# A phase's maxima turned by four VectorE transpositions instead of one TensorE transposition, with 24 tiles of exponentials and a new issue table

## The chip, the cores and the metric

The kernel runs on one core of one Trainium2 chip. The metric is device time in microseconds (us); lower is better. Before the change the median of three runs is 1726.11 us (1723.06 to 1726.36).

## What is computed

A layer normalisation of x (2048 tokens by 512) feeds two branches: softmax attention with 32 heads of 16 channels, and a gated feed-forward network of inner width 1792 (SwiGLU). The output is x plus the attention's result times a SiLU of the feed-forward's result. All is float32.

```python
xn = _layernorm(x)                                   # 2048 x 512
q, k, v = split(xn @ wqkv)                           # 32 heads, 16 channels
p = softmax(q @ k.T * 16 ** -0.5)                    # 2048 x 2048 for each head
s = (p @ v) @ wo
h = silu(xn @ w1) * (xn @ w3)                        # 2048 x 1792
g = silu(h @ w2)
out = x + s * g
```

## The kernel before

**Phases.** Two heads are a pair (`p`, 16 pairs) and 1024 query columns are a `half` (2 of them), so there are 32 phases. In each phase the kernel goes over all 2048 keys. Before a phase's exponentials can be taken, the row maximum of every query has to be known: `max_unit` (L380 on) multiplies 128 queries by 512 keys on one half of the array (L388) and VectorE reduces the 512 scores in PSUM to one maximum for each query (L390, tile `mp`). A phase has 64 of these products, 32 on each half of the array.

**Bringing the maxima to the exponentials.** `max_rows` (L393 on) is a generator with four steps, run once for each phase. Step 1: VectorE reduces the four part maxima of each query to one (`mx`, 128 queries by 16). Step 2: ScalarE writes them negated to `nm`. Step 3: TensorE transposes `nm` into a PSUM bank (L403, 16 rows by 128), ScalarE copies the rounded part to `mh` (L406) and VectorE writes the rest to `ml` (L407). Step 4: four transfers on SyncE's queue (SP, L414) write `mh` and `ml` of the two heads into rows 62 and 63 of each 64-row half of `qs`, the tile of queries. With these two rows the product of keys and queries already has the maximum subtracted.

**Exponentials and values.** `scores` multiplies keys by queries on one half of the array (L626), and ScalarE takes the exponential into a tile `pt` (L629), of which there are `PTS` = 23. `values` (L639) multiplies four such tiles with the values into the bank `pv`, 16 matmuls of 128 columns by 512 in the trace for two chunks of keys and 8 for one. The feed-forward network's products (L857, 4032 half-array products) run between them. All products but the values' go to seven PSUM banks in turn; `take` hands out the bank that the planner expects to be free first. GpSimd (POOL) splits and multiplies in SBUF for the feed-forward network (L320, L321, L727, L742, L744).

**The order of work.** The program is written out ahead of time: the string `ORDER_OF_ISSUE` has a letter for each piece of TensorE work, and the loop at the end of the kernel issues the pieces in that order. `f`, `m` and `s` are half-array products of the feed-forward network, the maxima and the scores (a capital is the upper half of the array), `v` is one chunk of values, `o` a tile of the final projection. In the table before, `r` is a `v` ahead of which `second` issues step 3 and step 4 of a phase's maxima, and `R` is that alone. A model in the kernel (`mod`) keeps an expected time for every engine; `small` uses it to choose where in the program the steps of `max_rows` are put. After the program is built the order on each engine is fixed, and a late engine is waited for.

Of the kernel before, what the change touches and what calls it, by code (L numbers as in the profile page):

```python
# [9 lines left out]
F32 = mybir.dt.float32  # L10
# [7 lines left out]
P = 128  # L18
# [17 lines left out]
PTS = 23  # L36
# [14 lines left out]
    "MfSfMffSMffSSffMfSffMfSfFFMMfffMMfsFfsFfFSffmFsFFfMsFfMFfmmFFmMFvvSmmFsFfSffMsFfmFFsFfMsfFSfMfFfMsFS"  # L51
    "ffMFfFffMFSfFfMfSfSfmsfFmFFsFmFsFfFmSfmFfFmMfFMmvvFsMMsFsfFfFmFsfFMsfFFmsFmFFfSffMfFfMMfFMfMfMsvvSmf"
    "MsfFfSFfmSFffSFmFmfFmSFffSFmFfFfMmfFMFmvvSmFmSffSfFmFmfFSfFsmFfFFsfFmFFfMfMfMfMFfFMmvvvsMsMfffFmFfSM"
    "fsFsFFffMsFFfmSFfFfFfmMFMfsMvrFSmmsFsFsFmFffFMfsFfMsfFfSMfSffMFfFfSffMfFMfSFFffMfSfsMfSFfmFsfFFmSFfm"
    "FsFfmFmFsFMsvvMsMmSsvFmsFMmmSvvmSSfMfFfSffMSffFmFFsSfmFFmFfsFfFSffMFmMmvvMsSffFfMfSfMfSFfmFFsmFfSfFF"
    "msFFsfFFsFmsMvvsMSmMsvMmfMSfmMFvvMFssfMffSfMfSFfmSFffSmfFsFFmSfFFmsFfFFffMfSfMffSMfFFsmFfFmfSfFSfFmF"
    "sfFFmFsfSFsFmvrvvMsSffMFfSffMSffFmSSFffFmsFffMFSffMsFfsFMfFmFFfsmFmMvFvsMsMMsvMmsMfFSSfvSmMsMsvSmffS"
    "MffSFfMfSfMffSmsfFmSFfSfmsFfFSmFfFFmFsFmfSsFFfmFfSFfmFsFmSfFMfFffFmMMmvvMsfMfSMsvMssMMsvmSFfMsFsfFFm"
    "fFSmFsFfmFFsFfMsfFsFmFSfFfMfFsfSmFsFfFMfSffFMsFfMfFffMfMMffMMmvvvSmmMSmvvSmmSFfSffFFmsFFmFsFfFmSfSfF"
    "mfFfMSsfFFmfSfFmFsFFmFsfFFmSffFsFMffMMmvrfMFMsMmMfvvvfMSfMfSffSfMffSfMFsfmFFsFmSfsFfFFmfFmSfFFsFmFsF"  # L60
    "fmFsFFmsFFFmFssFSsvvSmsSsSvvSmSmmSvmSFmsFFfFsFmfSFfMsfFfSFmfSfFMfSfSfFmfMFfFFmMvvsMsMsfFfFmFfMsfFsFM"
    "ffSfFMfSfFmSfFsFfFfmMMsvrsMMssMvMsSfMffSFffMFfmSfSFfmFFsFfmFsFfMsFfFfFmSFmmMvvmSsMMmvvsMsFFmFmFsFfFs"
    "fFSmfFSfMfFfSfMffSfFSmfFFffFFMSffMfFSffSmfsMfsFFmFsFmFsFmFfFMfmFMmvvMsMmfSfSvmSsMSmvMsfMfSfFSffMFfmS"
    "fSFfFmFfsFmsFfFSFmfSfFmfFfFMSFfffFSFmsFfmFFmsFfsFSffMFFffmFFfMmMmvvvvmMSsMsvSmsFmFmFFsFsFfFfSmFfSfMf"
    "FffMSffFsMfFfFMffSFfFMfSfSfFMfsmsFfFmsFfFMsFmFfSfmFfFFmfMMmvvvmSMssSvrvSmmFsFsFmFFsfFFfMsfFfMfSfFfMS"
    "mfFfSfFfMFsfMFMsvvvmFsFmsFFmsFFffSfMfSFfmSfFmFsFMffFSfSfMmvmSMffMsSvsMSfSffMFfFfSmfFsFMfsFfFsMFfFmsF"
    "sFfMFfffFMfSffSFMffMsfSFfFmFsfFMsfFmFsFFfFmFmFmSmvvvSmsSsSvvSsMmMsvfSfMSfMfSffMfSfFfSfMFfsFFsmFfsFMf"
    "sFfFMsFfmFSFfffMFMfssMvsFSFMmMsvrvMsfSMfffSfMSffMFffSmssfFMFfsFmfFsFFmfSFmfFSffSFmSFfFmsFFfmFsFfMsFM"
    "fFffSmFSmvvSmMsMmvvmMSfmSSfvSmmSMsvSmsFFmsFFfFmSffFSmfFSfMfSffFMsfFMfsFFfMfsFfFsMFffSMfSffFsMFfmFFsm"
    "FfFFfFFMmMmvvvMssmFsFsFmFffFFsMfFsMfFfSffMSffMFffSmFfSfFfMSfFmSfFfFmSfFmfFFfMmmMvvrMsmFFfSsvvvSmsFFm"  # L70
    "FsfFFfFmSfmFfSfFFsmFmFfSFfFsmFFsFfmSfFmFsFFsfFfSSfMsvvSssSmMvvvFmsFmFsFmFsFfFsFFmSffFMsfFfMSfMffFMff"
    "MSsvMfmSMfSsvmSsMSmvmSfSMfSfFffMmFfSfsFmFfFSFfFsmFfSmFffSFffmFFMFfSfmFsfFFsMFfFsmFsfFMsfFmFSfFfMfFmS"
    "fMmvvmMsSMsvsMFmFsFsmFFfFsfFMsfFfMSfFfMfSffMFsfFfMmFfMMmvvvMmmSsMvrMsSffMFfSffMSfFfmSffFSmFsFfMsfFFF"
    "msFmmFfFFmMFmvvsMsMfFfSffMsFfMfFFsmFsFFfsFmSFffMfSfffFfMFfSMffSfMfFsFFmFsFmSffFFmFsFmFfFmmFsMvvSmSmS"
    "mvfMMsSfSmvmSmSSmvmSFmFsFfFsfMFsfMfFsFMffSFfmSFffMsFfMFfsMfFMmvvMmmMsSvrmSfSmFFfFsFmsFFsFmfFSMfSfFfm"
    "SfFMfSfFffMfMFmMsvvvsMMffSfFfSfMSffFsMFfsFmFFsfFsMFffMsFfFsFffFMfMfFSffSfMSffFmSfFfSmFsFfFmFsFmFFsFm"
    "FsmFvvvvsMSmFffFsFfFSmfFSfMfSffFmSfFmFsFFffMFFfmSSmvvvMsFsfMfsFfFMfsFfFFmsFMfsFMffFFsMfFffMfSsMvmSfS"
    "MfFffSfMSffFsMfFfSMffFSfFmsFfMFsFffMsFFfFsfFSsSmvvSmmFSSsvvvSmmSMsvSfMfSfMffSfFSfMffSfMsfFmFsfMfSFfF"
    "sFmFsfMFsfFMfsFFsfMFfFsFmsFfFMfsFfMsFMfFffFsSMmvmMsMmSvvmMsSMmvrmSfSMffSFffMSffFsMFfSfMffSFfmFsFmFfF"
    "FsFmsFfFmSfFFsFmFsFfmSFfmFsFfFfMfMSfmsMSSvmFmvmSSmmMvvmFMmFmMmvvvmFsFFmsFFsFmFffSmFSffMfSfFmFSfSffMf"  # L80
    "SFffMSffFMfFsfMSfFfFmsFMfFfsSfFmMvMssMsMvrsMsFFsFmFmFfFsFfmFFmSffFFsFmSffFSfmFSfmFSffFmFSfFmFfmFmFmS"
    "vvMmsSSmvsMmFFssFsFFmfFfFfMfSfMFsfFfMSfFmFfsFfMMmvFvMsMmSsvfMMfSsMsvMsfSffMSffMFffSFmmFSfffSMFfsfFmF"
    "fsfFmFFsFFfMFsFFfmsFFSfmfSFfMFfsFfmFSfFmFMffmFsMvvMsSsmMvSmmFMmFmvvrSmSfmFfFsFFmSffMFsFffMfSfMfSFsFf"
    "fMffFfFFMSffMfSfSfMfSfFmFsfmFSFfsmFFfsFFssFFsmFvvvvsMsMmSvMsFfsMSffFfMfSfMfFsMFfsSfFfMfFFsmFsFFfmFfF"
    "fMfFSfMfSfSfmFffSFmFFsmsFfFFmSFffFmFFmmSmvvmSmSmSvvmSMmMsvvsMsFFmFsFfFmFsFfMfFsfMSfMfFfSfMfFsfFfFMfS"
    "ffMfSfSfFMFfsmFsFfMsfFmFsFFfMfSfmFmFfFsFsMvvSfSfsMfSvvvsMMfSffFSffMsfFfMSfFsFFmsFfFmsFFFfsmFfFMfFfSm"
    "SfFFmFfSfmFfSmFSfFfFmsFFmfFSsFfsMvvvmSsSSsvvmSsMsSvrsMffSMSfFffMfSfFmSfSfFmFFsFfmfFSmFfFsFfFfmFfMSff"
    "FSmFsFfMfFsFmFsFSfmFsFfMfMfFFfFmmSmvvvMsmFfSFfsFFmfSFffMsFFsMfFffSMfSfFfMsfFMfSffMFffFMmmMvvvMsmmMff"
    "MvFvSfMfSMfSfffSMffSmSfFfMsfFFMfsFFsfMsfFFMfFsfMFsffFMsFsFfMfFsFmFsFFmsFfMfFMsfFmMvvvmSSFfmffSFfMfSf"
    "FmSffFSmfFFfSmsFFmFsfFFFmsfFSfMFsFfmfSfFMFsffMSfFfFFmsFmMsvvvrvfSMfSffMfSffSMfSFfmFSffMSfFffMsFFfsMf"  # L90
    "sFFsMFffSFmFfFsmFFsfFmSFfFmsFsfFFFsmFSsvvvSmSssSvvmSmSSmvSmFsSmFmvmSfFSmFsFfFmfFsFmFsFFmsFfFsFMffSFm"
    "SfFfmFSffMFssFFfSfsFMmvvSssMmSvvSsSsMmvvMsSmmSvMssFFmsFmFfFsFfMfSfFfMFsMffSfFfMsFfMFfmFFMfSmvvmSMssf"
    "FfFFmMfFsfFFsFmfFSmFFsfMFfMfffSMffSmSvmMmSSmvrsMmFSfFfFsFmFsfFMffSMffSMfFfSfFmsFfFFsFfSsMsvvvFFmsMfs"
    "SfFFffMSffFmfSMffFSfmFFsFsfFMfFFfMffSfMSffFFfSmfFsFmFsFmfSFfFmsFFmfFfMmFSFmvvmSsmFFsFfFfsMFfFsfMFsFf"
    "MsfFMfSfFfFmfSMfmSFvMmSsmMvvmMsMmMvvfSfMSffMfSfSfmFsFfFmFFsfMsFmFFfsFfFMmMfFfmSvvsMMsMsvmSfSMffFSffM"
    "SffFmSfsFFmFmfFSfFsFmSFfFfffmFFMSFfMfFfsFmsFfFFsmsFfFMsfFmFSfFfmFMsfSfMmvrvSmSmmsMvvMMSmvmFFsmFFssFm"
    "FFffSfMSffFmSFfMfsFfFMfsFSfMFmvMsFSmMsvMfMsMsfSFvssMSmfFfmSffFSmFFfsMSffFMfsFFmfSFffMfMFmmMvvvsMSfMf"
    "FffSfMfSFfmSfFfSFmFfFsmFfSFmfFsfFFmFfMfSfFSfmFSffFsFMfFssFmFfFmFsFMfFfFmSfsSvvvSmSmmMvrsMSfMfFfSffMf"
    "SFfmFsfFMssFfFMfSFfmFsFfMFsffMSFffMfFfsSMmvsSmMsFMvvvvMffSMfSffMfSffSfMfSfmSFfMfFsfMfFSsFfFmSfFfmFFs"
    "fMsFFffSFmSfFmsFfFFmsFsFfFmFFmMmvvMmsMMmvvFsFmsfFmFSfFFsmSffFFfMSfsFfMfFsFmFsfFFFmsfFSFmFfSfmFSffMsF"  # L100
    "ffFMMfMfffMFMfMmvvvMFsmfSffSfMfSffSMfFsFmFFsFfSmfFSfmFfFFsmFfFsMffFSFmSffFmSfFmFsFfFMfsFMfSmvMmmMSsv"
    "vmMSmMsvrSmFmFssFFsFmfFFfFsMfsFFmFffSFmFsmFfFsFFfMsfFfMSfFfFsFfSmSsFvvvvmFsFmFsFmFsfFfSFmFsFfMsfFMfS"
    "fSffFfMMfsMFvsMFMfSfsSvSmMfsfSffMmFfsFFfSFmSfFfmFsFfMfFFsFmSmvvSsFSmSmvFvmSMfSfFMmvvmSSmsffFmSfFfMsF"
    "fFsMFsFfsMfFfMfSfFFffMsMmMvvMsfMfSfFMffSfsFMfFSffMFsfmFsFfFSmfFfsFFmFfFFMSfffMsfFfFSmsFFmFsfFFsMFfFs"
# [1248 lines left out]
```

## Time and profile before

| | before |
|---|---|
| median of 3 runs | 1726.11 us (1723.06 to 1726.36) |
| the profiled execution | 1724.77 us, of which 1723.0 us are its span |
| TensorE (PE) busy | 1715.4 us, 13236 matmuls |
| VectorE (DVE) busy | 1418.7 us |
| ScalarE (ACT) busy | 1240.6 us |
| GpSimd (POOL) busy | 766.5 us |

The times of a matmul's end are modelled in the trace, so for TensorE the starts are what is read: the distance between the starts of two products is what the first one really held up. A row of the timeline that joins several instructions gives the start of the first.

### The profile page before, as it was taken

Reading aid. Unit: us, or ns where it says so; the run is one execution under the profiler, and the core shown is the slowest. Engines: PE = TensorE matmul, PEld = TensorE weight load, DVE = VectorE, ACT = ScalarE, POOL = GpSimd, SP = SyncE. Lnnn points to the kernel's source line nnn. Section 1 sums busy time; section 2 is a strip of 40 time slices with the busy share of each in tenths; the row PEclk is TensorE's granted clock in tenths of the full one; section 3 lists DMA queues with packets and bytes.
Section 4 is the critical chain, followed back from the end, with each engine's and each line's share of the span. In section 5 each row is a group of like instructions: output and inputs, shape, how many; then the busy total and the mean of one; then the engine's idle time right before and its main releaser. Section 6 shows DMA issues by size and latency. Waiting matters only on the chain.

```text
span 1723.0 us, 35685 instructions
## 1 busy us (share of the span) xinstructions
PE 1715.4 (100%) x13236; PEld 1099.0 (64%) x13236; DVE 1418.7 (82%) x2349; ACT 1240.6 (72%) x2440; POOL 766.5 (44%) x793
## 2 busy tenths in 40 slices
PE   9999999999999999999999999999999999999998
PEld 7877766666556666666666666656666666564466
DVE  7567989898889889888789897799878888888835
ACT  4223787778877787787887778777787778778952
POOL 4102744365546542654464706661666156621201
PEclk9999999999999999999999999999999999999999
DMA  8757213232332312233322303133413223130632
GB/s 282 248 204 206 65 46 66 53 70 64 73 113 59 66 53 61 55 66 95 100 64 55 80 19 91 57 75 94 94 53 67 57 66 94 30 112 20 214 121 99
DMA packets 147374, 155.37 MB, mean 90 GB/s; under 512 B 42368, under 2 KB 101760, under 8 KB 144224
## 3 DMA queue, kind: packets, MB, share of 16 engines
q1 hardware_dynamic: 146336, 152.04, 32.2%
q8 instruction: 104, 1.70, 0.4%
q10 hardware_dynamic: 864, 1.05, 0.2%
q14 instruction: 70, 0.57, 0.1%
HBM read 107.97 MB, written 44.02 MB: 88 GB/s over the span
## 4 chain that ended last, share of the span: by engine, by line
PE 98%; DVE 1%; DMA 0%; issue 0%; POOL 0%; ACT 0%; SPq 0%; DVEq 0%; ACTq 0%; POOLq 0%
PE f L857 28%; PE pv L639 28%; PE m L388 16%; PE e L626 16%; PE m L506 2%; PE e L194 2%; PE e L198 2%; PE e L196 2%; PE o L194 1%; PE o L198 1%; PE o L196 1%; PE m L479 0%; PE m L403 0%; DMA qs<-ml 0%; PE o L1088 0%; DVE wr L1035 0%
## 5 line engine op out<-in xcount | busy, mean ns | idle before, releaser
L390 DVE TENSOR_REDUCE mp<-m 128x1 f32<-128x512 f32 x2048 | 1287.1, 683 | 204.3 <-PE m L388 130.0
L629 ACT ACTIVATE pt<-e 128x512 f32<-128x512 f32 x2048 | 1072.3, 606 | 280.0 <-PE e L626 161.2
L626 PE MATMUL e<-qs,ks 64*128 64x512 f32 x2048 | 709.0, 408 | 0.6 <-DMA qs<-ml 0.5
L388 PE MATMUL m<-ks,qs 62*128 62x512 f32 x2048 | 708.2, 416 | 0.1
L639 PE MATMUL pv<-pt,vt 128*17 128x512 f32 x4096 | 497.4, 595 | 0.0
L388 PEld LDWEIGHTS m<-ks,qs 62*128 62x128 f32 x2048 | 334.4, 184 | 158.7 <-DVE mp L390 52.5
L626 PEld LDWEIGHTS e<-qs,ks 64*128 64x128 f32 x2048 | 343.1, 184 | 125.8 <-DVE mp L390 33.7
L639 PEld LDWEIGHTS pv<-pt,vt 128*17 128x17 f32 x4096 | 90.2, 96 | 220.0 <-issue 210.2
L857 PE MATMUL f<-xth,wh 64*128 64x512 f32 x488 | 175.4, 392 | 0.0
L857 PE MATMUL f<-xtl,wh 64*128 64x512 f32 x488 | 174.6, 392 | 0.0
L857 PE MATMUL f<-xth,wl 64*128 64x512 f32 x488 | 173.2, 394 | 0.0
L742 POOL TENSOR_TENSOR h<-g,h 128x512 f32<-128x512 f32 x56 | 72.2, 1289 | 187.7 <-ACT h L738 187.6
L857 PE MATMUL f<-wh,hs 64*128 64x512 f32 x496 | 153.7, 393 | 0.0
L857 PE MATMUL f<-xtl,xeh 64*128 64x512 f32 x408 | 148.9, 392 | 0.0
L857 PE MATMUL f<-xth,xel 64*128 64x512 f32 x408 | 145.8, 395 | 0.0
L857 PE MATMUL f<-xth,xeh 64*128 64x512 f32 x408 | 142.4, 391 | 0.0
L857 PE MATMUL f<-xeh,hs 64*128 64x512 f32 x400 | 127.6, 393 | 0.0
L321 POOL TENSOR_TENSOR wl<-wr,wh 128x512 fp32r<-128x512 f32 x92 | 118.6, 1290 | 7.7
L320 POOL TENSOR_SCALAR wh<-wr 128x512 fp32r<-128x512 f32 x92 | 57.3, 622 | 121.2 <-PE f L857 61.2
L321 POOL TENSOR_TENSOR xel<-wr,xeh 128x512 fp32r<-128x512 f32 x76 | 98.0, 1290 | 6.3
L857 PEld LDWEIGHTS f<-xth,wl 64*128 64x128 f32 x488 | 85.4, 185 | 7.3 <-issue 3.4
L857 PEld LDWEIGHTS f<-xth,wh 64*128 64x128 f32 x488 | 86.9, 185 | 4.9 <-issue 0.8
(184 smaller groups left out, 2007.6 us busy)
## 6 DMA issues: line engine op xcount, KB each, us to landing
wr<-in_B_w_dram SPq DMA_DIRECT2D x168, 256.0 KB
qs<-qk SPq DMA_DIRECT2D x186, 64.0 KB
ks<-qk SPq DMA_DIRECT2D x90, 128.0 KB
qk<-sh SPq DMA_DIRECT2D x32, 256.0 KB
qk<-sl SPq DMA_DIRECT2D x32, 256.0 KB
v<-vrow SPq DMA_DIRECT2D x16, 272.0 KB
xin<-in_A_x_dram SPq DMA_DIRECT2D x16, 256.0 KB
g<-part SPq DMA_DIRECT2D x16, 256.0 KB
```

The source lines that it names most:

```text
L194: nc.tensor.matmul(ps, lhs[1], rhs[0], start=first, stop=False)
L196: nc.tensor.matmul(ps, lhs[0], rhs[1], start=False, stop=False)
L198: nc.tensor.matmul(ps, lhs[0], rhs[0], start=False, stop=last)
L320: nc.gpsimd.tensor_scalar(hi, t, 1.0, 1.0, op0=ALU.mult, op1=ALU.mult)
L321: nc.gpsimd.tensor_sub(lo, t, raw(hi))
L388: nc.tensor.matmul(ps, qs[p % 2][64 * h:64 * h + KM, q0:q0 + P], ks[p % 2][64 * h:64 * h + KM, c * 512:(c + 1) * 512], start=True, stop=True)
L390: nc.vector.reduce_max(mp[p, half][:, h, qt, c:c + 1], ps, axis=AX.X)
L626: nc.tensor.matmul(ps, ks[p % 2][64 * h:64 * h + KR, k * P:(k + 1) * P], qs[p % 2][64 * h:64 * h + KR, q0:q0 + 512], start=True, stop=True)
L629: nc.scalar.activation(pt, ps, AF.Exp, scale=DH ** -0.5)
L639: nc.tensor.matmul(pv[32 * j:32 * j + VW, :], vt[2 * p // GH][:, key, 2 * p % GH + j % 2, :], pt, start=key < 2 if last else k == 0, stop= ...
L742: nc.gpsimd.tensor_mul(h2, g, h2)
L857: nc.tensor.matmul(ps, left[r], right[r], start=starts and lane == 0, stop=ends and lane == 1)
```

## The change

`nm`, `mh`, `ml`, the TensorE transposition and its PSUM bank go. ScalarE still writes the negated maxima, now rounded, into the columns `hi` of a 128 by 32 tile `both` whose 32 columns are ordered head, part (hi, lo), query tile. VectorE writes the remainder into the columns `lo` (one instruction with two SBUF inputs, `m` and `hi`), and then transposes each block of 32 partitions by 32 columns into `turned`, 32 rows by 128. One transfer for each head takes 16 of those rows to two rows of `qs`. There are four steps still; step 3 is now these five VectorE instructions.

`PTS` goes from 23 to 24. The planner's `small` books 0.85 us of VectorE for step 3, and takes step 3 like the other steps, when the expected time has come; `second` and the letters `r` and `R` go. In the prologue three steps of the first phase's maxima, not two, are issued at place 7 of the last block. The issue table is new throughout (8598 letters, before 8599). The letters `f`, `m`, `s`, `o` have the same counts in both tables; 482 `v` and 30 `r` become 512 `v`.

```diff
-PTS = 23
+PTS = 24
...
 ORDER_OF_ISSUE = (
-    "MfSfMffSMffSSffMfSffMfSfFFMMfffMMfsFfsFfFSffmFsFFfMsFfMFfmmFFmMFvvSmmFsFfSffMsFfmFFsFfMsfFSfMfFfMsFS"
...
-    "MomSMsSSMSvMsSsMSmvsMMSsmSvMsMsSsvMssSMsoSSsSsvvsMsSsMMvSsSsSsMvvSoMmSSsvMssMSmSvSmSSmsMvSmsSmsMMvSv"
-    "vSRososSoSsosSSsSsvvsSSsSsoosSsSsSvvvvSsSssSosSSssSvvosSSsoosSSsoooosoSvvSsSsSsvvSssSSsooosSsSovvvv"
+    "MSfffMSsfFMfsfMfMffSSfSffMfMffSfMfSfmFssFFmSFFfmFsFMfsFMfFsfMfFMsFfmMvvFFMsMsfsfFFmFfFsMffSfMsFFmfFS"
...
+    "MvSmmSSSmoSsSsMsvvMssMsMSvSmsSSmMvSmSsMMsvSMssMsMvSmsMSMsvmSsMSMsvsMMSsSmvmSSsSsSvvMmMmSsosSsSsSoovv"
+    "vSsSsSsosSsSsSvosoSsSvSsSssSvvsSSssSoSssSsSvvvvsSsSSsosSSssSvvsSsSSsoSsSsSsoosooSSsooSoosvvooovvvv"
 )
...
-        nm = keep.tile([P, 16], F32, tag="nm", name="nm", bufs=2)
+        both = keep.tile([P, 32], F32R, tag="nm", name="nm", bufs=1)
+        hi, lo = (both.rearrange("p (h n q) -> p h n q", h=2, n=2)[:, :, n, :] for n in range(2))
+        m = m.rearrange("p (h q) -> p h q", h=2)
         yield
-        nc.scalar.activation(nm, m, AF.Copy, scale=-1.0)
+        nc.scalar.activation(hi, m, AF.Copy, scale=-1.0)
         yield
-        i, ps = take("m")
-        begins = mod.whole(0.1, was_free[i] + mod.NOTICE)
-        nc.tensor.transpose(ps[:16, :P], nm, ident)
-        mh = keep.tile([16, P], F32R, tag="mh", name="mh", bufs=2)
-        ml = keep.tile([16, P], F32R, tag="ml", name="ml", bufs=2)
-        nc.scalar.copy(mh, ps[:16, :P])
-        nc.vector.tensor_sub(ml, ps[:16, :P], raw(mh))
-        free_at[i] = mod.work("dve", mod.work("act", begins + 0.5, 0.25), 0.28)
+        nc.vector.scalar_tensor_tensor(lo, m, -1.0, raw(hi), op0=ALU.mult, op1=ALU.subtract)
+        turned = keep.tile([32, P], F32R, tag="nt", name="nt", bufs=1)
+        for b in range(4):
+            s = slice(32 * b, 32 * b + 32)
+            nc.vector.transpose(raw(turned)[:, s], raw(both)[s, :])
         yield
         c = slice(half * 1024, (half + 1) * 1024)
         for h in range(2):
-            for n, v in enumerate((mh, ml)):
-                r = 64 * h + KM + n
-                nc.sync.dma_start(raw(qs[p % 2])[r:r + 1, c], raw(v)[8 * h:8 * h + 8, :])
+            r = 64 * h + KM
+            nc.sync.dma_start(raw(qs[p % 2])[r:r + 2, c], raw(turned)[16 * h:16 * h + 16, :])
...
-                for _ in range(2 if n == 7 else 1):
+                for _ in range(3 if n == 7 else 1):
                     next(first_rows, None)
...
-    def small(due=False):
+    def small():
         for c in list(rows):
-            if c[2] == 2 and not due or c[2] != 2 and c[0] > mod.now:
+            if c[0] > mod.now:
                 continue
             if c[2] == 0:
                 c[0] = mod.work("dve", mod.now, 0.25)
             elif c[2] == 1:
-                c[0] = mod.work("act", c[0], 0.2) + 1.0
+                c[0] = mod.work("act", c[0], 0.2)
+            elif c[2] == 2:
+                c[0] = mod.work("dve", mod.now, 0.85)
             if next(c[1], "end") == "end":
-                ready[c[3]] = mod.free["dve"] + 3.5
+                ready[c[3]] = mod.now + 4.5
                 rows.remove(c)
-            elif c[2] == 2:
-                c[0] = mod.now
             c[2] += 1
...
-    def second():
-
-        while rows and rows[0][2] < 2:
-            rows[0][0] = 0.0
-            small()
-        if rows:
-            small(True)
...
-        if c in "rR":
-            second()
-        if c in "rv":
+        if c == "v":
...
-        if rows and rows[0][2] == 2 and rows[0][0] <= mod.now:
-            second()
```

More of the change, by code (lines that the diff above doesn't have):

```diff
@@ L56 @@
[L56 to L80, printed above, removed]
@@ L1271 @@
                 late.append("o")
-        elif c != "R":
+        else:
             what = (c.lower(), int(c.isupper()))
```

141 lines of the change are left out of this document (83 added, 58 removed).

## The prediction

> **What bounds the kernel now.** I read the page first: the busy times, the TensorE line of the 40 slices, and the chain that ended last.
>
> ```profile
> span 1723.0 us, 35685 instructions
> PE 1715.4 (100%) x13236; PEld 1099.0 (64%) x13236; DVE 1418.7 (82%) x2349; ACT 1240.6 (72%) x2440; POOL 766.5 (44%) x793
> PE   9999999999999999999999999999999999999998
> PEclk9999999999999999999999999999999999999999
> PE 98%; DVE 1%; DMA 0%; issue 0%; POOL 0%; ACT 0%; SPq 0%; DVEq 0%; ACTq 0%; POOLq 0%
> ```
>
> TensorE is at work from end to end at the full granted clock, and the chain runs over it for 98%. A busy share alone proves little where the ends are modelled, so the groups of instructions come next: the last number is the idle time ahead of a group.
>
> ```profile
> L626 PE MATMUL e<-qs,ks 64*128 64x512 f32 x2048 | 709.0, 408 | 0.6 <-DMA qs<-ml 0.5
> L388 PE MATMUL m<-ks,qs 62*128 62x512 f32 x2048 | 708.2, 416 | 0.1
> L639 PE MATMUL pv<-pt,vt 128*17 128x512 f32 x4096 | 497.4, 595 | 0.0
> L403 PE MATMUL m<-ident,nm 128*16 128x128 f32 x32 | 8.9, 277 | 0.0
> ```
>
> None of TensorE's main kinds of work waited for anything worth naming. So the time is the sum of what TensorE is given to do, and every product that goes shortens it, as long as the other engines keep up. What a product holds up is read from the timeline of TensorE, as distances between starts.
>
> ```profile
> 560.67 1.91 PE L639 MATMUL pv<-pt,vt 128*17 128x512 f32 x16
> 562.51 0.50 PE L626 MATMUL e<-qs,ks 64*128 64x512 f32 x1
> 563.09 0.39 PE L626 MATMUL e<-qs,ks 64*128 64x512 f32 x1
> 563.41 1.05 PE L639 MATMUL pv<-pt,vt 128*17 128x512 f32 x8
> 564.40 0.49 PE L857 MATMUL f<-xtl,wh 64*128 64x512 f32 x1
> 564.73 0.39 PE L626 MATMUL e<-qs,ks 64*128 64x512 f32 x1
> 564.96 0.39 PE L857 MATMUL f<-xth,wh 64*128 64x512 f32 x1
> 576.51 1.05 PE L639 MATMUL pv<-pt,vt 128*17 128x512 f32 x8
> 577.50 0.28 PE L403 MATMUL m<-ident,nm 128*16 128x128 f32 x1
> 577.71 1.05 PE L639 MATMUL pv<-pt,vt 128*17 128x512 f32 x8
> 578.69 0.50 PE L388 MATMUL m<-ks,qs 62*128 62x512 f32 x1
> ```
>
> Two chunks of values in a row hold the array for 562.51 - 560.67 = 1.84 us, one for 564.40 - 563.41 = 0.99, so a chunk costs 0.85. With the transposition between them, two chunks hold it for 578.69 - 576.51 = 2.18 us. The transposition thus costs 2.18 - 1.84 = **0.34 us**, more than its own 0.21 to the next start.
>
> **The change part by part.**
>
> *The transposition goes.* 30 letters `r` of the old table put it beside values: 30 x 0.34 = 10.2 us; one of them follows a half-array product and not a chunk, so I take **-10.1 us**. The other two (prologue, and `R` near the end) stand among full-array products; I take nothing for them.
>
> *The new table.* I count both strings. Stretches of values without a break fall from 276 to 273 (a transposition inside one not counted as a break). A break costs, from the rows above, 564.96 - 563.09 = 1.87 us for one chunk and three steps of a half-array pair; a step is 564.96 - 564.73 = 0.23, so 1.87 - 0.85 - 0.69 = 0.33 us: three fewer, **-1.0 us**. Between two breaks the half with more products sets the length; summed over all stretches the longer half has 4119 products in the old table and 4115 in the new: 4 x 0.23 = **-0.9 us**.
>
> *The last phase.* In the old table the first score of the last phase stands at the end of its maxima, and that shows:
>
> ```profile
> 1635.96 0.22 DVE L396 TENSOR_REDUCE mx<-mp 128x16 f32<-128x64 f32 x1
> 1642.83 0.63 SPq L414 DMA_DIRECT2D qs<-ml  x1
> 1645.06 0.40 PE L198 MATMUL o<-ks,xth 128*128 128x512 f32 x1
> 1645.98 1.46 PE L626 MATMUL e<-qs,ks 64*128 64x512 f32 x6 [0.53 <-DMA qs<-ml]
> 1650.02 0.40 PE L198 MATMUL o<-ks,xth 128*128 128x512 f32 x1
> 1650.35 0.50 PE L626 MATMUL e<-qs,ks 64*128 64x512 f32 x2
> 1651.77 0.96 PE L626 MATMUL e<-qs,ks 64*128 64x512 f32 x6
> ```
>
> The step to 1645.98 is 0.92 us where the same step to 1650.35 is 0.33, and the six scores take 1.46 where six later ones take 0.96: 0.59 + 0.50 = 1.1 us lost to the transfer. The chain from `mx` to the first score is 1645.98 - 1635.96 = 10.0 us. In the new table the work between the last maximum of phase 31 and its first score adds up, with the prices above, to some 12 us, and the chain is shorter by two transfer issues of 0.63 and by TensorE's and ScalarE's part. I take **-1.1 us**. Bounds: 0 if something else is late there, -1.1. The nearest such place is phase 1, with some 8 us between; its chain is not queued behind the final loads, and I take nothing.
>
> *VectorE's five instructions.* This is the part with an unknown price.
>
> ```profile
> L390 DVE TENSOR_REDUCE mp<-m 128x1 f32<-128x512 f32 x2048 | 1287.1, 683 | 204.3 <-PE m L388 130.0 <-PE e L626 53.9 <-PE f L857 9.1
> L407 DVE TENSOR_TENSOR ml<-m,mh 16x128 fp32r<-16x128 f32 x32 | 8.7, 273 | 9.0 <-ACT mh L406 8.8
> L396 DVE TENSOR_REDUCE mx<-mp 128x16 f32<-128x64 f32 x32 | 7.0, 220 | 1.1
> L653 DVE RECIPROCAL rec<-sums 128x16 f32<-128x16 f32 x29 | 6.9, 238 | 0.0
> L461 DVE TENSOR_SCALAR ve<-mv 128x1 f32<-128x1 f32 x16 | 2.5, 154 | 0.6
> 300.00:1500.00 1200.00, 1200.00 (x9839) 758.15 (x9833) 1027.52 (x1691) 939.41 (x1844) 617.17 (x630) 1.00 0.28 69
> ```
>
> No row shows a VectorE transposition. The small instructions lie between 154 and 273 ns, so five are 0.77 to 1.37 us; each of the five depends on the one before or shares its tile, so I count whole durations: 5 x 0.20 = 1.0 us, nearest to the 220 of the reduction of 64 elements. The planner books 0.85. In the middle stage VectorE is busy for 1027.52 of 1200 us, 86%, so some 33 us more in the whole run do not make it the bound; what counts is lateness at the spot, when a bank is given back later than the order supposes.
>
> The remainder is also the first VectorE instruction of this stage with two SBUF inputs. What that can mean beside GpSimd, the end of the kernel shows:
>
> ```profile
> 1713.08 1.30 POOL L1035 TENSOR_TENSOR wr<-pt,wr 128x512 f32<-128x512 f32 x1 [0.23 <-DVE pt L1034]
> 1713.73 1.20 DVE L1035 TENSOR_TENSOR wr<-pt,wr 128x512 f32<-128x512 f32 x1
> L1035 DVE TENSOR_TENSOR x<-res,x x8: 691/691/693, 1659.7 to 1701.8; 128x512 f32<-128x512 f32 x8
> L490 DVE TENSOR_TENSOR wql<-wr,wqh x7: 682/685/1762, 5.9 to 29.8; 128x512 fp32r<-128x512 f32 x7
> ```
>
> The same addition takes 0.69 us alone and 1.20 when it starts inside one of GpSimd's; of L490's seven, one took 1.76. GpSimd is busy for 617.17 of 1200 us, 51%, so about every second remainder meets one of its instructions, with half of 1.30 us left on average: 0.51 x 0.65 = 0.33 us (bounds 0 and 1.30). The burst is then 1.0 + 0.33 = 1.33 us, **0.48 us** more than booked.
>
> How much of this reaches TensorE? Bounds: nothing, or all, 31 x 0.48 = 14.9 us. The nearest row is the reciprocal, L653: 238 ns, for which the planner books nothing at all, 29 times, and TensorE's idle time stays at the tenths shown. I stay near that end and take a quarter, 31 x 0.12 = **+3.7 us**. It would cost 14.9 if VectorE had no pause before the late bank is needed; its pauses ahead of L390 sum to 204.3 us, 6 us for a phase.
>
> The Trainium skill, "SBUF — State Buffer", section "SBUF: two separate sides", says that VectorE with two SBUF inputs and GpSimd reading SBUF exclude each other for a whole instruction. The rows of L1035 agree; by this rule alone the term of 0.33 stands, and a rule that both share the port would make it smaller. The skill's "VectorE: DVE Perf Modes", section "Two Vector instructions with no wait between them", says that an instruction whose input starts in another group of 32 partitions than the last one's is held until the earlier ones have finished; the four blocks start in four such groups, so none would overlap. With that page's formula for float32 the five would be an estimated 0.93 us, and the sum 0.07 x 31 / 4 = 0.5 us better; no row here shows it.
>
> *What costs nothing.* ScalarE loses the copy L406 and keeps the negation; TensorE does not wait for it. SP issues two transfers for four. `both` and `turned` have one buffer each, and the next phase's use is far off: 1723.0 us over 32 phases are 54 us each. In the prologue step 3 comes one place sooner; VectorE paused 2.15 us there for its old counterpart:
>
> ```profile
> 153.04 0.28 DVE L407 TENSOR_TENSOR ml<-m,mh 16x128 fp32r<-16x128 f32 x1 [2.15 <-ACT mh L406]
> ```
>
> In the loop, the remainder waits in VectorE's queue for ScalarE's `hi`, and the reductions behind it, which give back banks, wait with it; the old `ml` waited for `mh` in just this way, 8.8 us in all, without a gap on TensorE. The 24th tile lets scores run further ahead; values waited for none, so it is worth nothing but the order it allows, counted above.
>
> **The sum**: -10.1 - 1.0 - 0.9 - 1.1 + 3.7 = -9.4 us. Against the profiled execution's own 1724.77 us this is 1715.4; that execution lies 1.3 below the median of 1726.11, so the forecast could read up to 1716.7. I say **1715.5**.
>
> **The rivals.**
>
> *All is absorbed.* VectorE's lateness always falls into its pauses: -13.1 us, 1711.7. For it: the reciprocals. Against it: VectorE at 86% and five instructions in a row.
>
> *The gain is eaten.* The lateness passes whole to TensorE, -13.1 + 14.9 = +1.8: 1726.6; or the 0.34 us between two chunks turns out to be needed by ScalarE's exponentials, so that the chunks stay apart and only 3.0 us less 3.7 remain: 1725.5. Against the second: idle time ahead of L639 is 0.0.
>
> *Slower: the remainder meets GpSimd at the full length of its instruction nearly every time* (both engines run in a rhythm set by the same products): 1.30 + 5 x 0.25 = 2.55 us, 1.7 over the plan; half of it absorbed leaves 31 x 0.85 = 26 us, so 1724.8 - 13.1 + 26 = 1738. It decides from 13.1 / 31 = 0.42 us on that reach TensorE in each phase. For it: the 1.76 of L490. Against it: six of L490's seven took 0.69.
>
> **How the numbers follow.** My sum, with 1 to 7 us lost to VectorE, 1712 to 1719: 0.50. All absorbed: 0.20. Eaten: 0.14. Slower: 0.16. Less than 0.2% (3.4 us) is about what a measurement can't tell from no change: faster 0.70, same 0.14, slower 0.16. The range from 1710 to 1728 leaves out the slower rival and holds the rest; the likeliest case alone is 1711 to 1720.
>
> **What would show it.** Right: no L403 among TensorE's groups, two chunks of values always 1.84 us apart from the next product, idle times of TensorE's groups near zero, no step over 0.4 us ahead of the last phase's scores. Wrong: steps between half-array products well over 0.23 us behind a remainder, a remainder over 0.5 us long, transpositions well over 0.25 us, or idle time of L388 and L626 that names VectorE.

## The result and the profile after

| | before | after |
|---|---|---|
| median | 1723.79 us (six runs, 1723.06 to 1726.36) | 1718.05 us (six runs, 1716.68 to 1718.99) |
| span of the profiled execution | 1723.0 us | 1717.2 us |

The ratio is 0.9962, with a 95% interval from 0.9949 to 0.9975: the changed kernel is faster, by some 5.7 us. (The three runs shown ahead of the prediction are among the six.) The forecast was 1715.5, so the time lies 2.5 us above it and inside the range. The gain is further off: 9.4 us were forecast, counted from an execution of 1724.77, and 5.7 came; 1.0 us of the difference is that the median before, with three more runs, is 1723.79.

The page of the changed kernel, first the span and the busy times, then the groups that answer to those shown of before:

```profile
span 1717.2 us, 35614 instructions
PE 1709.9 (100%) x13204; PEld 1095.6 (64%) x13204; DVE 1445.2 (84%) x2477; ACT 1232.4 (72%) x2408; POOL 764.5 (45%) x793
...
L390 DVE TENSOR_REDUCE mp<-m 128x1 f32<-128x512 f32 x2048 | 1286.2, 683 | 171.8 <-PE m L388 87.3
...
L624 PE MATMUL e<-qs,ks 64*128 64x512 f32 x2048 | 719.8, 410 | 0.2
L388 PE MATMUL m<-ks,qs 62*128 62x512 f32 x2048 | 710.5, 416 | 1.8 <-ACT pt L627 1.6
L637 PE MATMUL pv<-pt,vt 128*17 128x512 f32 x4096 | 491.9, 595 | 0.0
```

TensorE has 32 matmuls fewer (13236 to 13204) and VectorE 26.5 us more work (1418.7 to 1445.2). TensorE's groups still show almost no idle time, but there is one new entry: 1.6 us ahead of L388 that end with ScalarE's exponential. Nothing in the change was to touch that wait.

The new instructions, each with shortest, median and longest duration, first and last start:

```profile
L403 DVE SCALAR_TENSOR_TENSOR nm<-mx,nm x32: 164/176/1179, 150.8 to 1633.7; 128x16 fp32r<-128x16 f32 x32
L407 DVE STREAM_TRANSPOSE nt<-nm x128: 198/199/204, 151.0 to 1634.6; 32x32 f32<-32x32 f32 x128
L412 SPq DMA_DIRECT2D qs<-nt x64: 610/653/810, 152.8 to 1635.5; - x64
```

A transposition takes 0.20 us, as assumed. The remainder takes 0.18 us, and up to 1.18.

**Where the 5.8 us of the two spans went.** Counted from the starts of all products in both traces: the transposition's steps -10.25 us (stretches of values and transpositions together 342.33 before, 332.08 after); the longer halves 3 products fewer, -0.7; the step ahead of the last phase's first scores -0.6 (the other 0.5 us of that wait lay inside a stretch and is counted among the small waits); the main stage begins at 159.83 us instead of 160.38, -0.55; the final stage is 0.6 shorter; a pause just behind the start of the main stage, **+3.5**; and small waits spread over the half-array products, **+3.7**. They sum to -5.5; the other 0.3 us are not placed. By a small wait I mean what a stretch of half-array products takes, from its first start to its last, beyond 0.239 us for each step of its longer half: 0.23 for the step, and the first step of a stretch, which takes 0.34, spread over all of them (which product runs on which half is known from the program). They are 14.8 us in all before and 22.0 after, 3.9 of these at the start, where before had 0.4. These totals hang on that allowance; the differences between kernels hardly do. The idle column shows almost none of them, because a matmul is shown busy for 0.39 us where the next one normally starts 0.23 after it: a wait of up to 0.16 lies inside.

The pause at the start, in the timeline of the changed kernel (SP's queue, TensorE, ScalarE):

```profile
160.55 0.32 SPq L510 DMA_DIRECT2D v<-vrow  x1
...
161.54 0.39 PE L855 MATMUL f<-xth,xeh 64*128 64x512 f32 x1
163.53 0.50 PE L388 MATMUL m<-ks,qs 62*128 62x512 f32 x1 [1.59 <-ACT pt L627]
...
162.88 3.54 ACT L627 ACTIVATE pt<-e 128x512 f32<-128x512 f32 x7 [2.24 <-DMA v<-vrow]
```

TensorE stops from 161.54 to 163.53 because the first exponential, which gives back a bank, has not run. ScalarE waits for a transfer, `v<-vrow`, that has nothing to do with its scores. The product counts put this pause and the crowding behind it at 3.5 us.

The longest remainder, in phase 2, and the wait behind it; GpSimd, VectorE and TensorE (I call the five VectorE instructions of step 3 a burst):

```profile
255.36 1.28 POOL L725 TENSOR_TENSOR g<-th,g 128x512 f32<-128x512 f32 x1
...
255.50 1.18 DVE L403 SCALAR_TENSOR_TENSOR nm<-mx,nm 128x16 fp32r<-128x16 f32 x1
256.71 0.84 DVE L407 STREAM_TRANSPOSE nt<-nm 32x32 f32<-32x32 f32 x4
257.49 3.03 DVE L390 TENSOR_REDUCE mp<-m 128x1 f32<-128x512 f32 x5
...
256.80 1.05 PE L637 MATMUL pv<-pt,vt 128*17 128x512 f32 x8
257.78 0.50 PE L388 MATMUL m<-ks,qs 62*128 62x512 f32 x1
258.18 0.49 PE L624 MATMUL e<-qs,ks 64*128 64x512 f32 x1
258.18 0.49 PE L388 MATMUL m<-ks,qs 62*128 62x512 f32 x1
258.77 0.50 PE L624 MATMUL e<-qs,ks 64*128 64x512 f32 x1
...
259.11 0.39 PE L624 MATMUL e<-qs,ks 64*128 64x512 f32 x1
```

The remainder starts inside GpSimd's L725 and ends with it; all 14 remainders longer than 0.2 us begin inside a GpSimd instruction and end 0.02 to 0.03 us behind its end. The burst holds VectorE for 257.49 - 255.50 = 1.99 us instead of 0.98, and TensorE's six half-array products behind it, three on each half, take 1.33 us from the first start to the last where 0.57 would do: 0.76 us lost, of which the idle column shows nothing.

The last phase:

```profile
1631.43 0.22 DVE L396 TENSOR_REDUCE mx<-mp 128x16 f32<-128x64 f32 x1
...
1641.63 0.96 PE L624 MATMUL e<-qs,ks 64*128 64x512 f32 x6
...
1645.17 0.40 PE L198 MATMUL o<-ks,xth 128*128 128x512 f32 x1
1645.50 0.97 PE L624 MATMUL e<-qs,ks 64*128 64x512 f32 x6
```

Its first six scores take 0.96 us, as undisturbed ones do, against 1.46 before. Now 10.2 us lie between `mx` and the first score, and the last transfer is issued at 1635.5, 6.1 us ahead of it.

### The profile page after: what moved, and what is told of

Read it like the earlier page. It is cut to its first block, busy times and chain, and to the rows that moved or that the text cites. A ratio compares the mean times of both kernels' runs of the same rounds, so it can differ in the third digit from the quotient of the medians.

```text
span 1717.2 us, 35614 instructions
## 1 busy us (share of the span) xinstructions
PE 1709.9 (100%) x13204; PEld 1095.6 (64%) x13204; DVE 1445.2 (84%) x2477; ACT 1232.4 (72%) x2408; POOL 764.5 (45%) x793
## 3 DMA queue, kind: packets, MB, share of 16 engines
q10 hardware_dynamic: 864, 1.05, 0.2%
## 5 line engine op out<-in xcount | busy, mean ns | idle before, releaser
L624 PE MATMUL e<-qs,ks 64*128 64x512 f32 x2048 | 719.8, 410 | 0.2
L388 PE MATMUL m<-ks,qs 62*128 62x512 f32 x2048 | 710.5, 416 | 1.8 <-ACT pt L627 1.6
L637 PE MATMUL pv<-pt,vt 128*17 128x512 f32 x4096 | 491.9, 595 | 0.0
L388 PEld LDWEIGHTS m<-ks,qs 62*128 62x128 f32 x2048 | 335.9, 184 | 158.7 <-ACT pt L627 46.3
L624 PEld LDWEIGHTS e<-qs,ks 64*128 64x128 f32 x2048 | 346.5, 185 | 134.2 <-DVE mp L390 35.1
L855 PE MATMUL f<-xth,xeh 64*128 64x512 f32 x408 | 146.6, 395 | 0.0
L724 POOL TENSOR_SCALAR th<-th 128x512 f32<-128x512 f32 x56 | 34.6, 618 | 127.9 <-ACT th L717 127.8
L855 PE MATMUL f<-wl,hs 64*128 64x512 f32 x248 | 91.4, 392 | 0.0
```

What stands on the lines that cost most here:

```text
L388: nc.tensor.matmul(ps, qs[p % 2][64 * h:64 * h + KM, q0:q0 + P], ks[p % 2][64 * h:64 * h + KM, c * 512:(c + 1) * 512], start=True, stop=True)
L624: nc.tensor.matmul(ps, ks[p % 2][64 * h:64 * h + KR, k * P:(k + 1) * P], qs[p % 2][64 * h:64 * h + KR, q0:q0 + 512], start=True, stop=True)
L637: nc.tensor.matmul(pv[32 * j:32 * j + VW, :], vt[2 * p // GH][:, key, 2 * p % GH + j % 2, :], pt, start=key < 2 if last else k == 0, stop= ...
L724: nc.gpsimd.tensor_scalar(th, th, 1.0, 1.0, op0=ALU.add, op1=ALU.mult)
L855: nc.tensor.matmul(ps, left[r], right[r], start=starts and lane == 0, stop=ends and lane == 1)
```

## The experiments

All were timed beside the kernel before, whose median was 1723.4 to 1723.8 us in these comparisons; the ratios are against it. From the first experiment on, most start from the changed kernel with the `gap` of the first, so that the pause at the start is out of the way; their differences are taken against it.

**1. Memory at the start.** The 24th tile makes the pool `work`, opened behind the prologue, 2 KB larger. In the memory layout of the two programs it ended at byte 183712, just under the prologue's `pros`, which begins at 183872; now it ends at 184224 and reaches over `vrow`, which begins at 182336, and whose transfer must then end before the pool can be used. An unused tile in the pool below moves `pros` up to 184384.

```diff
+        pro.tile([P, 512], F32, name="gap")
```

> The changed kernel with one unused tile of 2 KB in the prologue's pool, so that the pool `work` (24 tiles of exponentials) no longer reaches into the memory of the pool `pros`, whose last transfer stores a row of values at about 160.5 us. Theory (memory): the first exponential waits for that transfer only because the two pools overlap; the pause of some 2 us on TensorE at 161.5 us and the slow products behind it go, no step of over 0.5 us between half-array products is left in the first 10 us of the main loop, and the time falls by 3.5 us, from 1718.05 to about 1714.5. Rival (chain): the pause comes from the first phase's maxima, whose steps stand one place sooner; then nothing changes, 1718.

Measured: **1714.6 us** (1714.36 to 1714.95), ratio 0.9947 [0.9935, 0.996], 3.45 us under the changed kernel. Page and ScalarE's timeline:

```profile
span 1712.8 us, 35613 instructions
...
L388 PE MATMUL m<-ks,qs 62*128 62x512 f32 x2048 | 710.8, 416 | 0.1
...
160.25 6.15 ACT L628 ACTIVATE pt<-e 128x512 f32<-128x512 f32 x12
```

The first exponential starts at 160.25 and not 162.88, and the 1.6 us ahead of L388 are gone. So the pause came from an overlap of memory, not from the new table or from the transpositions. Only the kernel of experiment 2, which passes on the maxima rounded, is faster in this study.

**2. The remainder's second input.** The columns `lo` are filled with zeros by an instruction with one input and about the same length (157 to 163 ns); the remainder is left out.

```diff
+    none = const.tile([P, 16], F32, name="none")
+    nc.gpsimd.memset(none, 0.0)
...
-        nc.vector.scalar_tensor_tensor(lo, m, -1.0, raw(hi), op0=ALU.mult, op1=ALU.subtract)
+        nc.vector.reduce_max(raw(both).rearrange("p (h n q) -> p h n q", h=2, n=2)[:, :, 1, :],
+                             none.rearrange("p (h q o) -> p h q o", h=2, o=1), axis=AX.X)
```

> As gap, and the remainder of the maxima is left out: VectorE writes zeros into its columns with a reduction of one input, so that no VectorE instruction of step 3 has two SBUF inputs (the maxima then reach the scores rounded). Theory (collision): the two longest waits of TensorE in the middle of the changed kernel, 0.76 us at 258 and 1.02 us at 1444 us, follow the two remainders that met a GpSimd instruction and took 1.18 and 1.16 us; both go, and the time is 1.5 to 2.5 us below gap, about 1712.5. Rival (length): it is the five instructions in a row, 0.98 us without any collision against 0.85 booked, that cost a little in every phase; then the time is at most 0.7 us below gap.

Measured: 1713.95 us (1713.6 to 1713.97), ratio 0.9942 [0.9929, 0.9956]: 0.65 us under `gap`, where 1.5 to 2.5 was expected. The long remainders are gone, and with them the two waits of 0.75 and 1.05 us that stood behind the two longest, but the small waits in all fell only from 18.1 to 17.7. The time is what the rival forecast; its cause, the length of the burst, is tried in experiment 9. Meeting GpSimd costs this kernel some 0.65 us in all, not the larger part of the 3.7. It may be a little more: a burst that meets nothing is 0.05 us longer here (1.03 for 0.98, because the first transposition starts 0.25 us behind the instruction ahead of it and not 0.20), 1.5 us of VectorE in 31 phases that stand against the gain.

**3 and 4. More VectorE time at the spot.** Each transposition is issued twice (eight for a phase, 0.84 us more), or two of the four are (six, 0.42 us more). What is computed stays the same.

```diff
         for b in range(4):
             s = slice(32 * b, 32 * b + 32)
             nc.vector.transpose(raw(turned)[:, s], raw(both)[s, :])
+            nc.vector.transpose(raw(turned)[:, s], raw(both)[s, :])
```

> As gap, with each of the four transpositions done twice: 4 x 0.21 = 0.84 us more of VectorE in each of 32 phases, not booked by the planner. It measures which share of a lateness of VectorE reaches TensorE. A quarter, as forecast: 31 x 0.84 x 0.25 = 6.5 us above gap, about 1721. Absorbed in VectorE's pauses: less than 1.5 us above gap. Passed on whole: 26 us above gap, 1740.

> As gap, with two of the four transpositions done twice: 0.42 us more of VectorE in each phase, half of what eight_turns adds. In eight_turns 0.84 us more in 31 phases cost 19.4 us, a share of 0.74. Theory (there is a small reserve at each place, and what goes beyond it is passed on whole): less than half of 19.4, 5 to 8 us above gap, 1720 to 1722.5. Rival (a fixed share of every lateness is passed on): 9.7 us above gap, 1724.3.

Measured: eight 1733.97 us (1.006 [1.0047, 1.0073]), 19.4 over `gap`; six 1722.03 (0.9991 [0.9982, 0.9999]), 7.4 over it. Of the time added in 31 phases (26.0 and 13.0 us) TensorE lost 0.74 and 0.57: far more than a quarter, and a larger share the more there is. The view that shows it is that of the waits of TensorE's weight loads, which run ahead of the products and are the first to miss a bank (waited for, total us, times, longest us). Of `gap`, of six, of eight:

```profile
PEld m L388 <- DVE mp L390: 43.3, 74, 0.9
PEld e L625 <- DVE mp L390: 36.4, 64, 0.9
```

```profile
PEld m L388 <- DVE mp L390: 46.2, 81, 0.9
PEld e L626 <- DVE mp L390: 39.3, 73, 0.9
```

```profile
PEld m L388 <- DVE mp L390: 51.7, 99, 1.0
PEld e L626 <- DVE mp L390: 47.5, 90, 1.2
```

Together 79.7, 85.5 and 99.2 us: 5.8 and 19.5 more, about what the spans grew by (6.8 and 19.3) and the small waits (from 18.1 to 25.0 and 37.0). VectorE gives its banks back later and TensorE pays. With these three kernels the order of work is the same; experiments 5 and 8 show that the view does not compare kernels of different order.

**5. The old table with the new path.** The changed kernel with `gap` and the old issue table, its `r` read as `v`.

```diff
 ORDER_OF_ISSUE = (
-    "MSfffMSsfFMfsfMfMffSSfSffMfMffSfMfSfmFssFFmSFFfmFsFMfsFMfFFsfMfFMsFfmMvvFFMsMsfsfFFmFfFsMffSfMsFFmfFS"
+    "MfSfMffSMffSSffMfSfMfSfFFMMfffMMfsFfsFfFSffmFsFFfMsFfMFfmmFFmMFvvSmmFsFfSffMsFfmFFsFfMsfFSfMfFfMsFS"
...
```

> As gap, with the table of before (each r made a v, R left out) in place of the new one: what the new table is worth by itself. As I count the pieces in the order in which they are really issued (a letter that cannot be served is issued late), both tables have 270 breaks by values, and the longer half has 4073 products in the old and 4070 in the new. Theory (the table matters little): 0.7 us for the halves and about 1 us at the last phase, so 0.5 to 2.5 us above gap, about 1716. Rival (the table carries the gain, or the burst of VectorE needs it): 5 us or more above gap, 1719.5 or more.

Measured: 1738.63 us (1736.44 to 1738.88), ratio 1.0084 [1.007, 1.0097], **24.0 over `gap`** (the profiled execution, whose trace is read here, took 1736.44, and its span is 21.5 over that of `gap`). The theory that the table brings only its fewer breaks and shorter halves fell. In the trace the breaks (269) and the longer halves (4077 products) are nearly those of `gap` (270 and 4070); what grows are the waits, the small ones from 18.1 to 35.6 us, 20.5 of them in stretches behind a burst where `gap` has 3.7. The weight loads of `old_table`:

```profile
PEld m L388 <- DVE mp L390: 61.7, 103, 0.9
PEld e L625 <- DVE mp L390: 42.7, 76, 1.3
```

104.4 us against 79.7: 24.7 more. Between two tables this view is a hint only: before the change the same loads waited 86.2 us (52.5 and 33.7) and after it 78.6 (43.5 and 35.1), while the small waits rose from 14.8 to 22.0. Where a burst starts, the two tables differ too: on average 0.93 products of maxima have begun and not yet come to VectorE in the old one, 0.30 in the new one, and in the 2.5 us from its start on TensorE has 0.58 chunks of values in the old and 1.19 in the new. A chunk takes 0.85 us and needs no bank from VectorE.

**6. The transposition's price.** `gap` with TensorE's transposition of the maxima put back into step 3; its result is not read.

```diff
+        flat = m
...
+        i, ps = take("m")
+        begins = mod.whole(0.1, was_free[i] + mod.NOTICE)
+        nc.tensor.transpose(ps[:16, :P], flat, ident)
+        free_at[i] = begins + 0.5
```

> As gap, with one TensorE transposition of the phase's maxima put back into step 3, into a bank of its own; nobody reads it and nobody waits for it. It measures the price of the transposition by itself. Of its 31 places in the main order 21 stand beside values and 10 among half-array products, and the longer halves grow from 4070 to 4077 products, 1.6 us. Theory (the transposition holds the array for 0.2 to 0.34 us each time): 31 x 0.2 to 0.34 = 6 to 10.5, and 1.6: 8 to 12 us above gap, 1722.5 to 1726.5. Rival (it stood where TensorE had nothing to lose, and the table made the gain): less than 3 us above gap.

Measured: 1728.39 us (1727.52 to 1729.52), ratio 1.003 [1.0018, 1.0041], 13.8 over `gap`. Its small waits are those of `gap` (17.7 us against 18.1); the cost is in the steps around the transpositions, in ten stretches of values more (280), and in a start 1.75 us later (161.14 against 159.39). The term of -10.1 fits as TensorE's own time; here ten of the 31 places stand among half-array products and the start is later, so it costs a little more.

**7. The old table with the burst where the transposition was.** As 5, but `r` and `R` are kept, and `second` issues step 3 there.

```diff
+        if c in "rR":
+            second()
-        if c == "v":
+        if c in "rv":
...
+        if rows and rows[0][2] == 2 and rows[0][0] <= mod.now:
+            second()
```

> As old_table (the old table, 24 tiles, VectorE's transpositions, the gap), but the five VectorE instructions are put where the old table's letters r and R stand, ahead of a chunk of values, as the old kernel did with its step 3, and not at the time that the planner expects. Theory (what matters is how many products of maxima already wait for VectorE when the burst begins: 0.93 on average in old_table, 0.30 in gap, 0.03 in the old kernel at its own step 3): the burst falls behind values again, most of the 24 us that old_table lost come back, and the time is 1714 to 1724. Rival (the old table is wrong for the new path for another reason, such as 24 tiles or letters issued late): within 6 us of old_table, 1732 or more.

Measured: 1735.96 us (1735.79 to 1737.46), ratio 1.0075 [1.0062, 1.0087], 21.4 over `gap`. My theory that only the place of the burst was wrong fell: with 0.40 products of maxima waiting at its start, not 0.93, the small waits are still 35.2 us, 15.0 behind bursts.

**8. The 24th tile.** The changed kernel with `PTS = 23`; without `gap`, since its pool does not reach over `vrow`.

```diff
-PTS = 24
+PTS = 23
```

> The changed kernel with PTS at 23 in place of 24, all else the same, no gap. It measures what the 24th tile is worth. With 23 tiles the pool `work` ends below the memory of `pros` of its own accord. Theory (the tile is worth nothing, as forecast, and its memory is what costs 3.5 us at the start): the pause at 161.5 us is gone and the time is that of gap, 1713.5 to 1716. Rival (the table needs 24 tiles): letters come late and it is 3 us or more above gap.

Measured: 1723.99 us (1723.15 to 1724.44), ratio 1.0002 [0.9993, 1.0011]: 9.4 over `gap`. The main stage begins at the same time to 0.01 us and the small waits are the same 18.1 us. What differs is the order really issued: a letter whose scores have no free tile is issued later, which leaves 287 breaks for 270 and longer halves of 4085 for 4070 products. With the prediction's prices this is 17 x 0.33 + 15 x 0.23 = 9.1 us. The tile is worth 9.4 us, by this count all by the order that it allows, and the price of a break holds. The theory that it is worth nothing fell. The weight loads wait 85.6 us for the maxima here (44.2 and 41.4), 5.9 more than in `gap`, though the small waits are the same: not every such wait is lost time.

**9. A shorter burst in the new table.** One transposition over all 128 partitions (0.21 us) takes the place of four; its blocks stay on their partitions, so eight transfers of short pieces bring them.

```diff
-        turned = keep.tile([32, P], F32R, tag="nt", name="nt", bufs=1)
-        for b in range(4):
-            s = slice(32 * b, 32 * b + 32)
-            nc.vector.transpose(raw(turned)[:, s], raw(both)[s, :])
+        turned = keep.tile([P, 32], F32R, tag="nt", name="nt", bufs=1)
+        nc.vector.transpose(raw(turned), raw(both))
...
-            nc.sync.dma_start(raw(qs[p % 2])[r:r + 2, c], raw(turned)[16 * h:16 * h + 16, :])
+            for b in range(4):
+                to = raw(qs[p % 2])[r:r + 2, c].rearrange("n (q b w) -> n q b w", q=8, b=4)[:, :, b, :]
+                nc.sync.dma_start(to, raw(turned)[32 * b + 16 * h:32 * b + 16 * h + 16, :])
```

> As gap (new table, 24 tiles), with one VectorE transposition over all 128 partitions in place of four; it leaves the four blocks on four groups of partitions, so eight transfers of 128-byte pieces bring them in place of two of 512-byte pieces. VectorE's burst falls from 0.98 to about 0.40 us; the last transfer of a phase is issued some 3.8 us later. Theory (behind the new table little of the burst reaches TensorE): 0.5 to 1.5 us gained from VectorE, and 0 to 5 us lost where a phase's first scores follow its transfers closely (phases 1, 2, 3 and 30): 1713 to 1719. Rival (the burst still costs the 3 us of waits by which gap stands above the old kernel's): 1711.5 or less, if the transfers cost nothing.

Measured: 1717.29 us (1717.17 to 1718.31), ratio 0.9965 [0.9951, 0.9978], 2.7 over `gap`. The groups and timelines of VectorE, SP and TensorE:

```profile
L405 DVE STREAM_TRANSPOSE nt<-nm 128x32 f32<-128x32 f32 x32 | 6.8, 211 | 1.7 <-DVE nm L403 0.5 <-DMA o<-ol 0.2
L625 PE MATMUL e<-qs,ks 64*128 64x512 f32 x2048 | 718.3, 409 | 1.1 <-DMA qs<-nt 0.9 <-issue 0.2
...
154.79 5.40 SPq L412 DMA_DIRECT2D qs<-nt  x8
...
162.06 0.49 PE L388 MATMUL m<-ks,qs 62*128 62x512 f32 x1
```

The 2.7 us are all in the prologue: the eight transfers hold SP's queue for 5.4 us, and the main stage begins at 162.06 and not 159.39. From there to the end of the span both take 1553.4 us. The scores wait 0.9 us for the later transfers, so in the new table the burst's last 0.6 us, 18 us of VectorE in 31 phases, cost about a microsecond at most. That the table has reserved them, as the planner's 0.85 us for step 3 would have it, fits this and is not shown by itself.

**10. The shorter burst in the old table** (5 with the edit of 9).

> As old_table (old table, 24 tiles, VectorE's transpositions), with the single transposition and eight transfers of one_turn. In old_table TensorE waits for some 20 us in the stretches behind a burst, by my count of steps between products, against 3.7 in gap. Theory (the old table has no room behind the burst; the burst is what it loses by): with a burst of 0.40 in place of 0.98 us most of it goes, and the transfers take back up to 5: 1719 to 1728. Rival (the old table is wrong for the new path for a reason that has nothing to do with the burst): less than 6 us gained, 1733 or more.

Measured: 1730.1 us (1728.92 to 1731.49), ratio 1.0037 [1.0024, 1.0049], 8.5 under `old_table`, although its main stage begins 2.2 later (161.91 against 159.68): between 9 us (profiled executions) and 11 us (medians) less from the start of the main stage on. Its weight loads wait 93.5 us for the maxima (57.6 and 35.9), 10.9 less. The time lies between what theory and rival forecast. In the old table the length of the burst counts, and explains not quite half of what that table loses.

**11. The shorter burst, placed as in 7.**

> As held (old table, 24 tiles, step 3 at the letters r and R), with the single VectorE transposition and eight transfers of one_turn: the burst falls from 0.98 to 0.40 us; the old kernel had 0.27 us of VectorE there. one_turn showed that the eight transfers delay the start of the main loop by 2.7 us. Theory (the length of the burst is what the old table has no room for): held's waits behind a burst, 15 us by my count, nearly all go, and the time is 1736 - 13 + 2.7 = 1722 to 1727. Rival (the old table lacks the pause that TensorE's own transposition gave the other engines): at most half of the waits go, 1730 or more.

Measured: 1739.68 us (1738.98 to 1740.17), ratio 1.0095 [1.0078, 1.0111], 3.7 over `held`. Some 2 us are the start (162.07 against 160.03). The rest of the expected gain met a new wait:

```profile
L625 PE MATMUL e<-qs,ks 64*128 64x512 f32 x2048 | 713.7, 411 | 5.0 <-DMA qs<-nt 4.3 <-ACT pt L628 0.7
```

The scores wait 4.3 us for the eight transfers, which come late there. So this run does not test the length of the burst cleanly: the weight loads' wait for the maxima did shrink, from 106.0 to 100.7 us, and the transfers took as much.

**12. Pause and burst together** (7 with the unread transposition of 6, ahead of the burst, among values as before the change).

> As held, with one TensorE transposition put back into step 3, as in with_turn, unread; with the letters r it stands beside values again, as in the old kernel. In the new table this transposition cost 13.8 us. Theory (behind the old table the pause of the transposition is time in which VectorE and ScalarE catch up, so that it costs less than its price): 0 to 6 us above held, 1736 to 1742. Rival (the pause is of no use to them): 10 to 14 us above held, 1746 to 1750.

Measured: 1742.09 us (1740.38 to 1742.99), ratio 1.0106 [1.0091, 1.0122], 6.1 over `held`, at the edge of what the theory allows, where the same instruction costs 13.8 in the new table. Its steps cost 10.9 us, about as they did before the change, and the main stage begins 1.2 us later, but the small waits fall from 35.2 to 28.9 us. So in this order 6.3 of the 10.9 us come back as smaller waits. That the other engines catch up while TensorE pauses for 0.34 us fits this and is argued: taking the pause away in an unchanged order would then free less than its length. This kernel also has the old order, the old transposition and the new VectorE instructions: beside before, its small waits are 28.9 against 14.8 us.

## Why the prediction came out right, and which steps did not

**The whole.** Without the overlap of memory the kernel is 9.0 us faster than before (1714.6 against 1723.64), and the sum was -9.4. In part this is luck: the term of the table promised 1.2 us too much, and the sum lacks 1.6 us that were gained, 1.0 by a main stage that begins sooner in `gap` and 0.6 by a shorter final stage.

**The transposition (-10.1).** Right: -10.25 by the steps, and 13.8 when it is put back less well placed.

**The new table (-1.9).** The price of a break is right (experiment 8), the count is not. I counted the letters of the table; a letter that cannot be served is issued later, some 180 to 190 of 8600, and in the traces both kernels have 270 stretches of values. The breaks gave 0 and not -1.0, the halves -0.7 (4073 to 4070) and not -0.9. More important is what the sum left out: the table is a plan for this one path. The same path in the old table costs 24.0 us more, so "table" and "path" cannot be priced apart. In the old order, time that VectorE is given in addition seems to reach TensorE nearly whole: 16.3 us from the start of the main stage on between before and experiment 12, whose main differences are the burst and the 24th tile, for some 0.6 us more of VectorE in each of 32 phases (0.98 and on average 0.16, against 0.27 and 0.28 of waiting for `mh`), 19 us in all. No run has the old table, the burst and 23 tiles, so this is not shown.

**The last phase (-1.1).** Right; the wait is gone.

**VectorE's five instructions (+3.7).** The size came out, +3.7 us of small waits away from the start (4.2 without the 0.5 that the last phase lost), but not by its working, and that they are VectorE's doing is not shown. The burst without a collision takes 0.98 us (1.0 assumed). The collision adds 0.16 on average, not 0.33: 14 of 32 remainders are over 0.2 us, near the every second one that I took, but they lose less. So the lateness over the 0.85 booked is 0.29 us and not 0.48. And the quarter is no constant: of the burst's last 0.6 us a microsecond at most reaches TensorE in all phases together (experiment 9), of what is added 0.57 and then 0.74 (experiments 4 and 3). Collisions are worth some 0.65 us (experiment 2). What the remaining 3 us of small waits are due to is not shown; that the new table by itself runs that much tighter fits experiment 9, but is only argued.

The Trainium skill, "SBUF — State Buffer", section "SBUF: two separate sides", bears on the collision: the remainder of 1.18 us against 0.18, which ends as GpSimd's instruction ends, and its absence when the second input is taken away, agree with its rule. Its "VectorE: DVE Perf Modes", section "Two Vector instructions with no wait between them", agrees as well: four transpositions of blocks from four partition groups take 0.84 us, 0.21 from start to start with 0.20 long each, so none overlapped. The estimate of 0.93 us from that page (0.94 when it is worked out again) compares with 0.98.

**"What costs nothing".** This is the step that failed, and it made the forecast 2.5 us too low. I counted buffers and instructions there, and not addresses: the 24th tile pushed a pool over memory that the prologue still used, +3.5 us, shown by experiment 1. Without it the time is 1714.6, 0.9 under the forecast.

**The 24th tile, "worth nothing but the order it allows".** Values did not wait for tiles, as I said, but the order it allows is worth 9.4 us, and I had not counted it: "counted above" was the table's letters, which are the same with 23 tiles. Without the tile the change would have been worth nothing (1.0002).

**The rivals.** "All is absorbed" gave 1711.7; the nearest, `no_second_input`, stands at 1713.95. "Eaten" and "slower" did not come about in the new table; the slower one's threshold of 0.42 us reaching TensorE in each phase is passed by eight transpositions, 19.4 / 31 = 0.63 (ratio 1.006). The old table ended there too (1738.63), but not by the mechanism that I named: its remainders meet GpSimd no oftener (10 of 32 over 0.2 us, 14 in the new table).

**What stays open.** Why the old table loses so much with the new path. The length of the burst explains 9 to 11 of its 24 us; its place alone does not (7), and the pause of the transposition covers some 6 (12). The transfers' delay spoiled the run that was to join the two (11), and the 24th tile was not taken out of the old table.

## What to carry to other kernels

When a buffer is added, look at where its pool ends in memory and what lived there before: an engine then waits for a transfer that has nothing to do with its data, as ScalarE did here for `v<-vrow`. Where the program's order is planned ahead, price a new instruction against the time that the plan reserves for it, since taking 0.6 us off the burst gained next to nothing here and what was added to it cost 0.57 to 0.74 of itself, and count the order that is really issued, not the table. Read waits of a pipelined TensorE from distances between starts and, between kernels of one order, from the waits of its weight loads; the idle time of its matmuls showed 0.2 us for the scores where all half-array stretches together had 22.0.

## What the runs showed of the hardware that I had not expected

One transposition of 128 partitions by 32 columns takes 211 ns, one of 32 by 32 takes 199: four blocks cost little more than one, and the blocks' place is then left to the transfers. Each of those holds SP's queue for 0.60 to 0.81 us, the short ones as long as the long ones, so eight for two cost 2.7 us where the queue is on the path.

A remainder that meets GpSimd can grow from 0.18 to 1.18 us, but 18 of 32 stayed at 0.2 us or less with GpSimd busy for 606.92 of the 1200 us of the middle stage:

```profile
300.00:1500.00 1200.00, 1199.81 (x9853) 755.75 (x9853) 1059.01 (x1812) 936.59 (x1827) 606.92 (x620) 1.00 0.28 69
```

Here the third time is VectorE's: 1059.01 us, 31.5 more than before, and still no bound by itself.
